# Late table clears, plain first-batch routing steps, and a reordered first expert group in an attention, expert and dense-FFN kernel

## The chip, the cores and the metric

One core of one Trainium2 chip runs the whole program. The metric is the device time of one execution in microseconds. Three runs of the kernel before gave 405.20, 402.61 and 406.21 us, median 405.2. The engines are PE (matrix), DVE (vector), ACT (scalar), POOL (GpSimd) and SP, which here issues nearly all DMAs.

## The reference

```python
r = log1p(|i - j|) / log1p(max(i, 1))                       # 576 x 576
bias = relu(r[..., None] @ w1 + b1) @ w2                    # 32 hidden -> 8 heads
attn = softmax(q @ k.T / 8 + bias)                          # 2 batches, 8 heads, head size 64
x = (attn @ v), heads side by side                          # 1152 tokens x 512

e = argmax(x @ w_gate); gate = softmax(x @ w_gate)[e]       # 8 experts, capacity 288
# token i gets the next place of expert e; past the capacity its row stays 0
y = relu(x_e @ w1[e]) @ w2[e]                               # 512 -> 1024 -> 512
x[i] = gate[i] * y[place of i]

h = x @ w_in                                                # 512 -> 2048
out = (max(h, 0) + alpha * min(h, 0)) @ w_out               # 2048 -> 512
```

## The kernel before

**Attention** (0 to about 209 us) is the function `course`. Its PE, ACT and DVE instructions stand in the order in which the program is written (`tc.manual_schedule`); the order of SP's DMAs and of POOL is left to a scheduler. The bias of a block of rows is made on the way: `h` on ACT and DVE (L164, L166), `bps` on PE (L174), `st` on ACT (L182), which SP writes to a table `bd` in DRAM (L188) and reads back sheared as `bias` (L138). Attention itself runs in 24 steps over pairs of heads and row blocks: scores `sps` on PE (L242), bias and row maximum `p`, `mn` on DVE (L249), the exponential on ACT (L256), transposes (L284), values `av` (L301, L302). The table `LD` tells which loads each step issues; what has been written there later stands later in SP's queue, and SP works its queue in order.

**Clears.** Expert input rows lie in a DRAM buffer `xd`, output rows in `out`. Before anything is scattered into them they are cleared from a tile `zr` of zeros: four DMAs into `xd` (L122) and three into `out` (L125), one in each of the steps 12 to 18 (L905, L906). POOL fills `zr` at the very start (L114, L115). In step 12 the constants `c` are loaded too (L907); DVE copies five columns of them into `gt` at L435.

**Routing** of one batch is a list of 14 steps (`routing`, L337 to L455): `logits`, `logits_rows`, `choose`, `highest`, `hot`, `ranks`, `slots`, `places`, `gates`, five `row` steps and `scatter`. `ranks` multiplies on PE into `rk` (L393 to L395), which takes one of the two PSUM buffers that `layer1` uses. `row` transposes a row block on PE (`xp`, L442), scales it on DVE (`xr`, L444) and copies gate and token beside it (L446). `scatter` writes the rows to their places in `xd` with POOL's indirect DMAs (L450). Every step is wrapped in `first(...)`, which gives what it issues a high priority. Batch 0 is routed inside attention, batch 1 in the first expert group.

**The first expert group** is `job` (L560), about 210 to 250 us: eight rounds `f`, each `layer1(f)` (12 matmuls, L572), ACT's `hh` (L574) and DVE's `hl` (L575), and 24 matmuls of `layer2(f-1)` (L582) that need them. The weights of a quarter are split into a high half on ACT (L501) and a low half on DVE (L502). `side(i)` calls what hangs at position `i`: batch 1's routing, then `joblist`, which on DVE (L459 to L494) makes the table `jl` of the groups that follow, then four conversions of dense-FFN weights (`ahead`: load L720 or L723, ACT L731, DVE L733 to L735). What follows needs `jl`: SP's loads of the next group's weights (`raw`, L512, L514) and rows (`xj`, L544), PE's transposes of those rows (`xjT`, L554), POOL's early split of the next weights (L533, L534). In this stage the scheduler orders all engines by priority and by its own times. Then come a second group with a rider (250 to 285 us) and the dense FFN (285 to 405 us).

Of the kernel before, what the change touches and what calls it, by code (L numbers as in the profile page):

```python
# [10 lines left out]
F32 = mybir.dt.float32  # L11
# [11 lines left out]
N, DM = B * S, H * D  # L23
# [5 lines left out]
RW = DM + 2  # L29
FEW = 96  # L30
TINY = 32
BIG = float(1 << 20)
# [7 lines left out]
def build(tc, nc, a):  # L40
    V, A, G, T, SY = nc.vector, nc.scalar, nc.gpsimd, nc.tensor, nc.sync
    with contextlib.ExitStack() as ctx:
# [5 lines left out]
        gp = pool(ctx, "gp")  # L48
# [61 lines left out]
        go, pick = c1[:, 346:386], c1[:, 386:450]  # L110
        c8v = c1[:, 136:176].rearrange("p (u e) -> p u e", e=8)
        wgb = c1[:, 218:346].rearrange("p (n e) -> p n e", e=32)
        zr = gp.tile([128, RW], F32, name="zr")
        G.memset(zr[:, 0:DM + 1], 0.0)  # L114
        G.memset(zr[:, DM + 1:RW], BIG)  # L115
        xd = dr.tile([XROWS, RW], F32, name="xd")

        def clear(r):

            if r < 12:  # L120
                n = XROWS // 12
                rows_of.other(SY.dma_start(xd[:].rearrange("(p r) w -> p r w", r=12)[:, r:r + 3],  # L122
                                           zr[0:n].unsqueeze(1).to_broadcast([n, 3, RW])))
            else:
                out_of.other(SY.dma_start(a["out"].rearrange("(p r) w -> p r w", r=9)[:, r - 12:r - 9],  # L125
                                          zr[:, 0:DM].unsqueeze(1).to_broadcast([128, 3, DM])))
# [178 lines left out]
        def first(f):  # L305
            with tc.high_priority():
                f()
# [29 lines left out]
        def routing(b):  # L337
# [101 lines left out]
            def row(u):  # L439
                t = ps1(pt, "xp")  # L440
                for hp in range(4):
                    T.transpose(t[:, 128 * hp:128 * hp + 128], xT[b][:, hp, 128 * u:128 * u + 128], ident)  # L442
                x = r.x[u] = raw.tile([128, RW], F32, tag="xr", name="xr", bufs=5)
                V.tensor_tensor(x[:, 0:DM].rearrange("p (h d) -> p h d", h=8), t.rearrange("p (h d) -> p h d", h=8),  # L444
                                r.rinv[:, u].unsqueeze(2).to_broadcast([128, 8, 64]), ALU.mult)
                V.tensor_copy(x[:, DM:RW], r.gt[:, u])  # L446

            def scatter():
                for u in range(5):
# [1 line left out]
                        out=xd[:], out_offset=bass.IndirectOffsetOnAxis(ap=r.ci[:, u:u + 1], axis=0),  # L451
                        in_=r.x[u], in_offset=None, bounds_check=XROWS - 1, oob_is_err=False))

            return [lambda f=f: first(f) for f in (logits, logits_rows, choose, highest, hot, ranks, slots, places, gates)
                    + tuple(lambda u=u: row(u) for u in range(5)) + (scatter,)]  # L455

        jl = gp.tile([128, 52], I32, name="jl")

# [90 lines left out]
        def job_transpose(ts, x, few=None):  # L549
            xh, xl = x  # L550
            for r in range(3):
                t = ps1(pt, "xjT")
                for d in range(4):
                    T.transpose(t[:, 96 * d:96 * d + 96], ts[r][:, 128 * d:128 * d + 128], ident[:96, :96])  # L554
                t = t[:, :384].rearrange("p (d r) -> p d r", d=4)
                halves(xh[:, :, 96 * r:96 * r + 96], xl[:, :, 96 * r:96 * r + 96], t)
                if few is not None and r == 0:
                    V.tensor_copy(few, t)

        def job(x, w0, raws, yo, side, engs=(None,) * 3):  # L560

            xh, xl = x
            acc = [pq.tile([128, 2, 512], F32, tag="pq", name="acc") for _ in range(2)]
            W = {0: w0}

            def layer1(f):
                w1h, w1l = [w.rearrange("p (k c) -> p k c", k=4) for w in W[f // 2][:2]]
                c = 128 * (f % 2)
                ps = ps1(pa, "g1")[:, :CAP]
                for k in range(4):  # L570
                    for i, (w, x_) in enumerate(((w1h, xh), (w1h, xl), (w1l, xh))):
                        T.matmul(ps, w[:, k, c:c + 128], x_[:, k], start=k + i == 0, stop=k + i == 5)  # L572
                hh, hl = [M.p.tile([128, 608], F32R, tag=n, name=n, bufs=3)[:, :CAP] for n in ("hh", "hl")]
                A.activation(hh, ps, AF.Relu)  # L574
                V.scalar_tensor_tensor(hl, ps, 0.0, hh.bitcast(F32), ALU.max, ALU.subtract)  # L575
                return hh, hl

            def layer2(f, hh, hl):
                w2h, w2l = [w.rearrange("p (f n) -> p f n", f=2)[:, f % 2] for w in W[f // 2][2:]]
                for d in range(4):  # L580
                    for i, (w, h) in enumerate(((w2h, hh), (w2h, hl), (w2l, hh))):
                        T.matmul(acc[d // 2][:, d % 2, :CAP], w[:, 128 * d:128 * d + 128], h, start=f == 0 and i == 0,  # L582
                                 stop=f == 7 and i == 2)

            prev = None
            for f in range(8):
                if f == 0:
                    W[1] = raw_split(1, raws[0], engs[0])
                h = layer1(f)
                side(2 * f)  # L590
                if prev:
                    layer2(f - 1, *prev)
                side(2 * f + 1)
                if f == Q3 and callable(raws[2]):
                    raws[2] = raws[2]()
                if f in (2, 4):
                    W[f // 2 + 1] = raw_split(f // 2 + 1, raws[f // 2], engs[f // 2])
                prev = h
            layer2(7, *prev)
            to_dense(acc, yo, CAP)  # L600
# [268 lines left out]
        raw = None  # L869
        NU = len(SL)  # L870
        late = []

        def course():
# [20 lines left out]
            LD = {s: [] for s in range(NU + 1)}  # L894
            for s, *x in ((0, load_bias, 0, 0), (0, load_bias, 0, 1), (1, load_bias, 0, 2), (1, load_bias, 0, 3),
# [6 lines left out]
                          (18, load, 1, 0), (19, load_bias, 2, 0), (19, load, 1, 1), (20, load_bias, 3, 0),  # L902
                          (21, load_bias, 2, 1), (21, load_bias, 3, 1)):
                LD[s].append(x)
            for s in range(12, 19):  # L905
                LD[s].append((clear, 3 * s - 36))  # L906
            LD[12] += [(lambda: SY.dma_start(c1, a["c1"]),), (rest_sums, 0)]  # L907
            LD[22].append((rest_sums, 1))

# [15 lines left out]
            for s in range(NU + 1):  # L925
# [9 lines left out]
                u, w = us[-1] if us else None, ws[-1] if ws else None  # L935
# [50 lines left out]
                else:  # L986
# [4 lines left out]
                    if w and w.small:  # L991
                        turn(w, 0)()
                        b = [blocks(1)]
                        turn(w, 4)()
                    elif w:
                        turn(w, 0, 1, 2, 3)('A')
                        turn(w, 4)('D')
                        b = [blocks(1)]
                    else:
                        b = [blocks(1)]  # L1000
# [14 lines left out]
                if s == 13:  # L1015
                    right.close()
                    raw = ctx.enter_context(tc.tile_pool(name="raw", bufs=1, side="right"))
# [47 lines left out]
        def prepare(r, at=9, late=False):  # L1065

            g = Unit()
            g.r, g.few, g.t = r, M.x[r % 2 if isinstance(r, int) else 0], None

            def tiles():  # L1070
                g.ts, g.x = row_tiles(), x_tiles(r == 1 if isinstance(r, int) else 0)

            def rows():
                if late:
                    tiles()
                    g.t = raw_tile(expert_of(r), 0)
                job_rows(g.ts, row_of(r, [ET.SP]))

            if not late:
                tiles()  # L1080
            g.todo = (at, rows), (14, lambda: job_transpose(g.ts, g.x, g.few))
            return g

        def group(g, few, side=lambda i: None, begin=lambda: None):
# [21 lines left out]
        def counts():  # L1106
            J.mode = nc.values_load(jl[0:1, 51:52], min_val=0, max_val=2, skip_runtime_bounds_check_because="a course")

        g1 = prepare(1, late=True)
        step = stepper(*zip((0, 1, 2, 2, 2, 3, 3, 3, 3, 4, 4, 4, 5, 5, 5), routing(1)), (6, lambda: first(joblist)), (7, counts),  # L1110
                       *((9 + i, lambda i=i: ahead(i)) for i in range(PRE)), *g1.todo)
        job(x0, w0, J.t0[1:], 0, step)
# [111 lines left out]
```

## Time and profile before

| | us |
|---|---|
| runs | 402.61, 405.20, 406.21 |
| the profiled execution | 406.84, span 405.0 |
| PE busy in the span | 375.8 (93%) |
| DVE, ACT, POOL busy | 284.2, 235.9, 29.3 |
| mean granted clock of PE | 0.987 of 2.4 GHz |

PE is busy for 93% of the span, so little of the time is idle; the table of windows tells in which stretches PE stood or ran at the lower clock. A row of a timeline gives start, duration, engine, line, operation, output, inputs, shape and count, and in brackets how long the engine was idle just before and for whom it waited. SPq is SP's queue: its duration is that of the issue, not of the transfer.

### The profile page before, as it was taken

To read this page: it belongs to the slowest core of one execution; us is meant where nothing else is said; L and a number is where in the kernel's file an instruction comes from. 1 tells how busy PE (TensorE), PEld (TensorE's weight loads), DVE (VectorE), ACT (ScalarE), POOL (GpSimd) and SP (SyncE) were. 2 spreads that over 40 slices of the span, in tenths; PEclk is the share of its full clock that TensorE was granted. 3 is DMA by queue.
4 is the path that set the end of the run, shared out by engine and by line. 5 is a ranking of instruction groups with operands and counts; after the bars stand their busy time and mean duration, and the time that the engine had idled before them with its cause. 6 is when DMAs were issued, how large, how long until landed. Compare 5 with 4: busy or idle time off the path is not lost. (4 is left out here: it accounts for less than half of the span.)

```text
span 405.0 us, 7529 instructions
## 1 busy us (share of the span) xinstructions
PE 375.8 (93%) x2728; PEld 274.0 (68%) x2729; DVE 284.2 (70%) x687; ACT 235.9 (58%) x518; POOL 29.3 (7%) x48
## 2 busy tenths in 40 slices
PE   4999997999999999999987997999999999999993
PEld 2424563546666656656656997878889898887982
DVE  5987975665656656776748897605999989887540
ACT  4876786776557655464644345515667657656531
POOL 2000000000000000012010522002000000000004
PEclk9999999899999999999999899999999999999998
DMA  7998899998997271341458179485345664540003
GB/s 302 292 288 276 282 356 251 320 311 301 400 326 272 87 251 43 108 142 36 119 170 242 59 214 324 138 279 153 112 155 179 180 207 146 168 158 3 0 0 129
DMA packets 44010, 78.77 MB, mean 195 GB/s; under 512 B 7127, under 2 KB 21591, under 8 KB 43964
## 3 DMA queue, kind: packets, MB, share of 16 engines
q1 hardware_dynamic: 42780, 75.73, 57.8%
q0 software_dynamic: 1184, 2.48, 1.7%
q8 instruction: 23, 0.38, 0.4%
q14 instruction: 23, 0.19, 0.2%
HBM read 59.50 MB, written 20.09 MB: 197 GB/s over the span
## 5 line engine op out<-in xcount | busy, mean ns | idle before, releaser
L249 DVE CUSTOM_DVE_ANT_0 p<-sps,bias 128x576 f32<-128x576 f32 x72 | 51.9, 754 | 23.6 <-PE sps L242 14.0
L256 ACT ACTIVATE p<-p,mn 128x576 f32<-128x576 f32 x72 | 55.7, 775 | 17.4 <-DVE mn L249 17.4
L174 PE MATMUL bps<-h,c 128*32 128x512 f32 (+17 forms) x352 | 39.5, 500 | 10.6 <-DVE h L166 5.4
L263 ACT COPY PT<-t 128x512 f32<-128x512 f32 (+2 forms) x52 | 27.5, 531 | 36.3 <-PE t L284 35.4
L166 DVE TENSOR_SCALAR h<-c 128x528 f32<-128x528 f32 (+17 forms) x126 | 46.4, 442 | 0.2
L284 PE MATMUL t<-ident,p 128*128 128x128 f32 x288 | 43.1, 282 | 2.8 <-ACT PT L263 1.5
L284 PEld LDWEIGHTS t<-ident,p 128*128 128x128 f32 x288 | 31.0, 141 | 20.8 <-ACT PT L263 9.0
L242 PE MATMUL sps<-kqv 64*128 64x288 f32 x256 | 43.3, 430 | 0.0
L806 PE MATMUL fg<-yh,w1l 128*128 128x304 f32 x120 | 36.3, 302 | 0.0
L806 PE MATMUL fg<-yh,w1h 128*128 128x304 f32 x120 | 36.2, 302 | 0.0
L806 PE MATMUL fg<-yl,w1h 128*128 128x304 f32 x120 | 36.2, 302 | 0.0
L182 ACT ACTIVATE st<-bps,c 128x527 f32<-128x527 f32 (+35 forms) x72 | 31.9, 510 | 7.0 <-PE bps L174 5.8
L301 PE MATMUL av<-PT,kqv 128*64 128x256 f32 (+1 forms) x320 | 33.5, 349 | 0.0
L731 ACT ACTIVATE cv<-d 128x512 f32<-128x512 f32 x32 | 21.6, 674 | 16.4 <-DMA d<-in_wout 7.8
L301 PEld LDWEIGHTS av<-PT,kqv 128*64 128x64 f32 x320 | 20.5, 140 | 15.6 <-issue 10.2
L242 PEld LDWEIGHTS sps<-kqv 64*128 64x128 f32 x256 | 25.2, 186 | 8.0 <-issue 2.7
L818 PE MATMUL facc<-w2h,hh 128*128 128x512 f32 (+1 forms) x75 | 29.8, 397 | 0.4 <-ACT hh L501 0.4
L818 PE MATMUL facc<-w2h,hl 128*128 128x512 f32 (+1 forms) x75 | 29.8, 398 | 0.3 <-DVE hl L502 0.3
L818 PE MATMUL facc<-w2l,hh 128*128 128x512 f32 (+1 forms) x75 | 29.6, 394 | 0.0
L174 PEld LDWEIGHTS bps<-h,c 128*32 128x32 f32 x352 | 11.5, 112 | 25.2 <-DVE h L166 8.4
L303 DVE COPY xT<-av 128x256 f32<-128x256 f32 (+2 forms) x28 | 9.2, 327 | 23.1 <-PE av L302 23.0
L501 ACT CAST hh<-g 128x304 fp32r<-128x304 f32 x32 | 14.3, 445 | 16.0 <-DVE g L810 15.8
(200 smaller groups left out, 768.8 us busy)
## 6 DMA issues: line engine op xcount, KB each, us to landing
bias<-bd SPq DMA_DIRECT2D x24, 576.0 KB, 5.9
kqv<-in_kqv SPq DMA_DIRECT2D x14, 864.0 KB, 6.5
bd<-st SPq DMA_DIRECT2D x36, 295.5 KB, 5.5
raw<-in_ew SPq DMA_DIRECT2D x16, 512.0 KB, 6.4
d<-in_win SPq DMA_DIRECT2D x16, 512.0 KB, 3.8
d<-in_wout SPq DMA_DIRECT2D x16, 512.0 KB, 3.8
w<-in_ew SPq DMA_DIRECT2D x6, 512.0 KB, 8.2
xd<-zr SPq DMA_DIRECT2D x4, 722.8 KB, 7.3
```

The source lines that it names most:

```text
L166: V.tensor_scalar(h, tab[:, :n], psi[:, i:i + 1], 0.0, ALU.add, ALU.max)
L174: T.matmul(ps[32 * c:32 * c + 32, n0:n1], w2n, hs[c][:, n0:n1], start=True, stop=True)
L182: A.activation(st[:, o:o + src.shape[1]], src, AF.Copy, scale=rr[:, t:t + 1])
L242: T.matmul(u.sc[ul, h][0][:, nh, :288], q[p, 128 * ul:128 * ul + 128], k[p, 288 * nh:288 * nh + 288], start=True, stop=True)
L249: V.tensor_tensor_reduce(out.rearrange("p (a b) -> p a b", a=2), ps[:, :, :288], bias.rearrange("p (a b) -> p a b", a=2), -0.125, 3.0e38, ...
L256: A.activation(out, out, AF.Exp, bias=mn, scale=-1.0, accum_out=acc)
L263: A.copy(o, i)
L284: T.transpose(t[:, jl, 128 * i:128 * i + 128], u.P[ul][:, 128 * j:128 * j + 128], ident)
L301: T.matmul(o[p, :n], v[:, j, p], rhs(h, j), start=j == 0, stop=False, skip_group_check=True)
L731: A.mul(v, r[:, :, 1].bitcast(F32), 2.0 ** -112)
L806: T.matmul(ps, w[:, 128 * k:128 * k + 128], x[:, k, s], start=k + i == 0, stop=k + i == 5)
L818: T.matmul(acc[i][:m], h[:, r:r + m], w, start=f == 0 and j == 0, stop=f == NF - 1 and j == 2)
```

## The change

Five edits. (1) `zr` is no longer filled at the start: it is made in another pool at the first clear. (2) The clears hang at steps 14 to 20 instead of 12 to 18. (3) Batch 0's routing steps lose the priority wrapper, and of batch 1's steps `gates` and the five `row` steps do. (4) In `job` the split of weight quarter 1 is written behind `layer1(0)` and `side(0)`. (5) The next group's loads hang at position 8 instead of 9, and its transposes at 15 instead of 14.

```diff
-        zr = gp.tile([128, RW], F32, name="zr")
-        G.memset(zr[:, 0:DM + 1], 0.0)
-        G.memset(zr[:, DM + 1:RW], BIG)
+        zr = None
         xd = dr.tile([XROWS, RW], F32, name="xd")
 
         def clear(r):
 
+            nonlocal zr
+            if zr is None:
+
+                zr = raw.tile([128, RW], F32, name="zr")
+                G.memset(zr[:, 0:DM + 1], 0.0)
+                G.memset(zr[:, DM + 1:RW], BIG)
...
-            return [lambda f=f: first(f) for f in (logits, logits_rows, choose, highest, hot, ranks, slots, places, gates)
-                    + tuple(lambda u=u: row(u) for u in range(5)) + (scatter,)]
+
+            return [(lambda f=f: first(f)) if b and i not in (8, 9, 10, 11, 12, 13) else f for i, f in enumerate(
+                    (logits, logits_rows, choose, highest, hot, ranks, slots, places, gates)
+                    + tuple(lambda u=u: row(u) for u in range(5)) + (scatter,))]
...
             for f in range(8):
+                h = layer1(f)
+                side(2 * f)
                 if f == 0:
                     W[1] = raw_split(1, raws[0], engs[0])
-                h = layer1(f)
-                side(2 * f)
...
-            for s in range(12, 19):
-                LD[s].append((clear, 3 * s - 36))
+            for s in range(14, 21):
+                LD[s].append((clear, 3 * s - 42))
...
-            g.todo = (at, rows), (14, lambda: job_transpose(g.ts, g.x, g.few))
+            g.todo = (at, rows), (15 if late else 14, lambda: job_transpose(g.ts, g.x, g.few))
...
-        g1 = prepare(1, late=True)
+        g1 = prepare(1, 8, late=True)
```

In attention the orders of PE, ACT and DVE stay as they were. Three places move. Lines of the changed kernel are 4 to 6 higher: its L126 is L122 here, L192 is L188, L913 is L907, L448 and L450 are L444 and L446, L508 is L502, L581 is L575, L739 to L741 are L733 to L735.

SP's queue around the load of the constants `c`, before:

```order
L188 DMA bd_117<-st 16x8x591 x2
L122 DMA xd<-zr 120x3x514
L907 DMA c_110<-in_c 128x450
L320 DMA rs_104<-rs_106 64x4x1 x2
L188 DMA bd_117<-st 16x8x591 x2
L122 DMA xd<-zr 120x3x514
L138 DMA bias<-bd_117 128x2x576 x2
```

and now, with the place where the first clears stand:

```order
L192 DMA bd_114<-st 16x8x591 x2
L913 DMA c_110<-in_c 128x450
L324 DMA rs_104<-rs_106 64x4x1 x2
L192 DMA bd_114<-st 16x8x591 x2
L142 DMA bias<-bd_114 128x2x576 x2
...
L142 DMA bias<-bd_115 128x2x576
L142 DMA bias<-bd_114 128x2x576
L126 DMA xd<-zr 120x3x514
L142 DMA bias<-bd_115 128x2x576
L199 DMA kqv<-in_kqv 128x1728
L126 DMA xd<-zr 120x3x514
```

No clear stands ahead of the constants any more; the clears stand between later loads of bias and heads.

DVE in the first expert group, from the end of batch 1's row products to the first two `hl`, before:

```order
L434 RECIPROCAL gt_2565<-sg 128x5
L1039 TENSOR_SCALAR malpha<-alpha 128x16
L386 SCALAR_TENSOR_TENSOR run<-c_110,eu 128x40
L446 COPY xr<-gt_2565 128x2 x5
L575 SCALAR_TENSOR_TENSOR hl<-g_2461,hh 128x288
L575 SCALAR_TENSOR_TENSOR hl<-g_2500,hh 128x288
L403 SCALAR_TENSOR_TENSOR kept_120<-thr,rk 128x8
```

and now, from the routing's first product on:

```order
L368 TENSOR_TENSOR lgt<-lgr,rinv_2470 128x320
L581 SCALAR_TENSOR_TENSOR hl<-g_2453,hh 128x288
L371 TENSOR_REDUCE L<-lgt 128x40
L1045 TENSOR_SCALAR malpha<-alpha 128x16
L508 TENSOR_TENSOR w2l<-raw,w2h 128x1024
L376 TENSOR_REDUCE mx<-L 128x5
L581 SCALAR_TENSOR_TENSOR hl<-g_2500,hh 128x288
L378 TENSOR_TENSOR m<-L,mx 128x40
```

The two `hl` come ahead of the row products; three products now stand ahead of `kept` and two far behind it, in `joblist`.

DVE at the end of the same group, around the last three `hl`, before:

```order
L735 SCALAR_TENSOR_TENSOR cw<-d,cw 128x512
L734 SCALAR_TENSOR_TENSOR ah_2762<-cv,ah_2762 128x512
L733 TENSOR_SCALAR ah_2762<-cv 128x512
L502 TENSOR_TENSOR ah_2761<-cw,ah_2761 128x512
L735 SCALAR_TENSOR_TENSOR ah_2762<-d,ah_2762 128x512
L575 SCALAR_TENSOR_TENSOR hl<-g_2844,hh 128x288
L734 SCALAR_TENSOR_TENSOR ah_2762<-cv,ah_2762 128x512
L735 SCALAR_TENSOR_TENSOR ah_2762<-d,ah_2762 128x512
L575 SCALAR_TENSOR_TENSOR hl<-g_2880,hh 128x288
L502 TENSOR_TENSOR xl<-xjT,xh 128x4x96
```

and now:

```order
L581 SCALAR_TENSOR_TENSOR hl<-g_2798,hh 128x288
L739 TENSOR_SCALAR cw<-cv 128x512
L739 TENSOR_SCALAR ah_2779<-cv 128x512
L740 SCALAR_TENSOR_TENSOR cw<-cv,cw 128x512
L740 SCALAR_TENSOR_TENSOR ah_2779<-cv,ah_2779 128x512
L741 SCALAR_TENSOR_TENSOR cw<-d,cw 128x512
L741 SCALAR_TENSOR_TENSOR ah_2779<-d,ah_2779 128x512
L581 SCALAR_TENSOR_TENSOR hl<-g_2844,hh 128x288
L508 TENSOR_TENSOR ah_2778<-cw,ah_2778 128x512
L581 SCALAR_TENSOR_TENSOR hl<-g_2880,hh 128x288
L508 TENSOR_TENSOR xl<-xjT,xh 128x4x96
```

Six conversions stand in one run ahead of `hl(6)`; the last conversion's three operations moved from ahead of `hl(7)` to between the `xl`. SP's `d<-in_wout` load for that last conversion now stands behind the `raw` and `xj` loads instead of ahead of them.

## Rows read from the trace of the kernel before

**Rows 1.** Windows by stage: busy us of PE, PEld, DVE, ACT, POOL, clock, DMA share, GB/s.

```profile
57.00:84.00 27.00, 23.81 (x204) 13.41 (x200) 17.24 (x53) 19.00 (x44) 0.00 (x0) 0.94 0.96 288
209.00:252.00 43.00, 38.05 (x275) 35.23 (x271) 36.57 (x93) 18.72 (x31) 12.10 (x9) 0.96 0.64 193
```

**Rows 2.** Timeline of steps 12 to 14: start, duration, work, idle time before and releaser.

```profile
58.21 1.40 PE L242 MATMUL sps<-kqv 64*128 64x288 f32 x8
58.99 1.29 SPq L122 DMA_DIRECT2D xd<-zr  x1
60.33 0.45 SPq L907 DMA_DIRECT2D c<-in_c  x1
63.87 1.36 PE L242 MATMUL sps<-kqv 64*128 64x288 f32 x8
66.35 0.17 DVE L435 COPY gt<-c 128x5 f32<-128x5 f32 x1 [4.21 <-DMA c<-in_c]
68.82 0.88 PE L174 MATMUL bps<-h,c 128*32 128x400 f32 x8 [2.90 <-DVE mn L249]
74.06 1.24 PE L242 MATMUL sps<-kqv 64*128 64x288 f32 x8
```

**Rows 3.** DMA issues by name, 57 to 75 us: count, size, median us to landing.

```profile
xd<-zr SPq DMA_DIRECT2D x4, 722.8 KB, 7.3
```

**Rows 4.** Windows inside the stages: idle stretches, and those at the lower clock.

```profile
70.00:73.30 3.30, 3.30 (x25) 1.63 (x25) 2.16 (x6) 2.62 (x6) 0.00 (x0) 0.50 0.92 280
223.60:226.90 3.30, 3.30 (x16) 3.30 (x15) 2.98 (x12) 0.00 (x0) 0.51 (x1) 0.50 0.00 0
243.10:246.40 3.30, 1.07 (x10) 0.86 (x10) 3.23 (x3) 0.89 (x2) 2.20 (x1) 1.00 1.10 304
```

**Rows 5.** Timeline of the first expert group.

```profile
221.25 0.81 DVE L575 SCALAR_TENSOR_TENSOR hl<-g,hh 128x288 fp32r<-128x288 f32 x2
221.75 0.42 PE L393 MATMUL rk<-run,ones 128*128 128x40 f32 x2 [2.33 <-DVE hl L575]
227.62 0.46 DVE L575 SCALAR_TENSOR_TENSOR hl<-g,hh 128x288 fp32r<-128x288 f32 x1 [1.04 <-ACT hh L574]
235.56 0.18 DVE L494 CAST jl<-jlst 128x52 int32<-128x52 f32 x1
245.16 0.55 PE L554 MATMUL xjT<-ident,xj 96*128 96x96 f32 x4 [2.06 <-DMA xj<-xd]
245.77 0.45 DVE L575 SCALAR_TENSOR_TENSOR hl<-g,hh 128x288 fp32r<-128x288 f32 x1
249.87 0.30 PE L572 MATMUL g<-xh,w1h 128*128 128x288 f32 x1
```

**Rows 6.** POOL's split of the next weights and the DVE operations beside it.

```profile
241.51 1.04 POOL L533 CAST w1h<-raw 128x1024 fp32r<-128x1024 f32 x1 [7.79 <-DVE ah L735]
241.70 1.40 DVE L734 SCALAR_TENSOR_TENSOR ah<-cv,ah 128x512 int32<-128x512 int32 x1
242.64 2.66 POOL L534 TENSOR_TENSOR w1l<-raw,w1h 128x1024 fp32r<-128x1024 f32 x1
243.13 2.71 DVE L735 SCALAR_TENSOR_TENSOR ah<-d,ah 128x512 int32<-128x512 int32 x1
```

**Rows 7.** Other conversions by line: count, ns least, median, most, first and last start.

```profile
L733 DVE TENSOR_SCALAR cw<-cv x30: 415/420/573, 228.3 to 367.7; 128x512 int32<-128x512 int32 x30
L735 DVE SCALAR_TENSOR_TENSOR cw<-d,cw x30: 679/683/693, 232.2 to 372.8; 128x512 int32<-128x512 int32 x30
```

**Rows 8.** Line L188, the writes of the bias table: count, ns, first and last start.

```profile
L188 SPq DMA_DIRECT2D bd<-st x36: 517/524/897, 9.3 to 91.9; - x36
```

**Rows 9.** Window of attention at 100 to 120 us.

```profile
100.00:120.00 20.00, 19.50 (x160) 12.69 (x160) 11.48 (x30) 12.04 (x29) 0.58 (x2) 1.00 0.98 358
```

**Rows 10.** DMA issues by name, 95 to 150 us: count, size, median us to landing.

```profile
kqv<-in_kqv SPq DMA_DIRECT2D x7, 864.0 KB, 5.3
out<-zr SPq DMA_DIRECT2D x1, 768.0 KB, 9.6
```

## The prediction, made before the changed kernel ran

> **What bounds the kernel now.** PE is busy for 93% of the span, so time can only come back where PE stands, where it runs at the lower of its two clock levels, or where another engine holds it. I read the windows by stage first. From 57 to 84 us PE is busy 23.81 of 27.00 us at a granted clock of 0.94, and from 209 to 252 us 38.05 of 43.00 at 0.96, with DVE at 36.57 [rows 1]. These are the stretches the change touches. Inside the dense FFN and the second group it moves nothing that I can see, and I take them as unchanged.
>
> Then the timeline of steps 12 to 14. A step is the time from one first score matmul to the next. The step from 58.21 takes 5.66 us, the step from 63.87 takes 10.19 [rows 2]: 4.53 us too long. Two rows say why. DVE's copy of `c` columns into `gt` waits 4.21 us for the DMA of the constants, until 66.35; behind it on DVE stand `h` and the row maxima, so PE waits 2.90 us before `bps` at 68.82 [rows 2]. After that PE runs at half clock (0.50, that is 1.2 GHz) for about 3.3 us, with PE busy all of it [rows 4]; that is worth up to half, 1.65 us. 2.90 + 1.65 = 4.55, which fits the 4.53.
>
> Last, the timeline of the first expert group. PE waits 2.33 us at `rk` for `hl(0)`, which stands on DVE at 221.25 behind batch 1's row products; then PE runs at 0.50 from 223.6 to 226.9 [rows 4, 5]. Near the end PE waits 2.06 us for the rows `xj` [rows 5], without a fall of the clock behind it (1.00 in the window 243.1 to 246.4) [rows 4]. But DVE is nearly full there: 2.98 of 3.30 us in the half-clock stretch, 3.23 of 3.30 at the end [rows 4], and its largest wait after `rk` is 1.04 us [rows 5]. So in the second half of this group DVE sets the pace, and PE time won early is mostly lost again.
>
> **The change, part by part.**
>
> *Clears off the constants' queue.* The constants were issued at 60.33 behind one clear of `xd` issued at 58.99 [rows 2]; now they follow `bd` directly. The issue moves up by 1.34 us. The transfer ahead of them, 722.8 KB [rows 3], is 2.6 us at this stretch's 288 GB/s [rows 1]. So the constants land 1.34 us earlier if only the issue counts, 2.6 us if the DMA engines work in order of issue; I take 2.2, nearer the second, since the DMA share there is 0.96 [rows 1] and an issue in a full queue waits for the bytes ahead. DVE's 4.21 becomes about 2.0, and PE's 2.90 about 0.7. A pause of 0.7 us is much shorter than those of 2.33 and 2.90 that preceded the two half-clock stretches, and shorter than the 2.06 that did not [rows 2, 4, 5], so I let that stretch go as well, but count only 1.1 of its 1.65 us because ACT and DVE were busy 2.62 and 2.16 of 3.30 there [rows 4] and do not get faster with PE. **Attention: -3.3 us.** Bounds: -1.3 (issue only, clock still halves) and -4.5 (whole excess).
>
> *Clears at steps 14 to 20, `zr` made late.* Four transfers of 722.8 KB and three of 768 KB go from a full stretch into the one up to about 150 us. At 100 to 120 us the DMA engines are at 0.98 with 358 GB/s [rows 9], yet PE is busy 19.50 of 20.00 there, though one `out` clear with 9.6 us to landing already stands among the loads [rows 9, 10]. The heads' loads land after 5.3 us [rows 10] and are issued a step or more ahead. The loads also lose the clears that were ahead of them. I take 0. Bounds: -0.5 (the idle PE time in that window) and the slower rival below. POOL fills `zr` on an engine idle there, 0.58 of 20 us busy [rows 9]; what waits for it is SP, and that is the rival's place. The fill that goes from the start was on POOL alone and is worth 0.
>
> *Priorities of batch 0.* The order of PE, ACT and DVE in attention is that of the program and does not move: 0.
>
> *`gates` and row products of batch 1 lose priority; the split is written later.* `hl(0)` and `hl(1)` now stand right behind the routing's first product. PE's 2.33 us at `rk` goes: `rk`'s PSUM buffer is free early, and PE has 23 matmuls of `layer2` ahead of it instead of 2. What is late next is DVE. Up to `hl(7)` its list loses the three operations of the last conversion, which now stand among the `xl`: 0.42 + 0.68 + 0.68 = 1.8 us at their usual durations [rows 7]. Of its idle 1.04 us [rows 5] some goes too. `hl(7)` was at 245.77 and the next group began at 249.87 [rows 5]. So -1.8 to -2.8 for `hl(7)`. Part returns behind it: the same three operations now delay the last `xl`, which the next group's first matmuls need, and ACT's step for that conversion waits for a weight load that SP now issues behind the loads of the next group's weights and rows. Between +0.5 (all returned and PE slowed) and -2.8, I take **-1.5 us**, nearest to the shorter list less a little. The half clock after `rk` I don't add: DVE was full beside it.
>
> *Loads at position 8, transposes at 15.* `jl` was written at 235.56 [rows 5]. Two operations of 0.68 us and perhaps the 1.04 of waiting no longer precede it, so it is ready 1.4 to 2.4 us sooner, and `xj` with it. The wait of 2.06 for `xj` was hidden, as PE needed `hl(7)` at about the same time. Counted at 0; if it were not hidden it is part of the -2.8.
>
> Sum: -3.3 - 1.5 = -4.8 us. The profiled execution took 406.84 (span 405.0 and 1.8 around it), so 402.0 for such an execution. It lies 1.64 above the median of the three runs, 405.2; against that: **400.4 us**.
>
> **A rule that speaks against it.** POOL splits the next weights in 1.04 and 2.66 us, and the two DVE conversions beside it took 1.40 and 2.71 us [rows 6] where 0.68 is usual [rows 7]: 0.72 + 2.03 = 2.75 us lost. The second of them started at 243.13 and ended at 245.84, 0.54 after POOL's at 245.30 [rows 6], so it did not run beside it but behind it. The Trainium skill, page "SBUF — State Buffer", section "Who interferes with whom", says that a DVE instruction with two SBUF inputs and a GpSimd instruction that reads SBUF never overlap, and that the later one is blocked for the whole of the other. The trace agrees (0.54 us left to do against 0.68 alone). By the rule up to all of POOL's 3.7 us could fall on DVE rather than 2.75, and the sum would be -3.8.
>
> **Rivals.**
>
> *The blockade moves onto PE's path.* Before, the 2.75 us fell ahead of `hl(7)` while PE waited 2.06 us for `xj` anyway. With `jl` 1.4 to 2.4 us earlier, POOL's split starts earlier, beside the run of six conversions ahead of `hl(6)`: 2 x 0.42 + 4 x 0.68 = 3.6 us alone [rows 7], 6.3 with 2.75 on top. PE has 24 matmuls of `layer2` meanwhile, about 2.5 us (16 took 3.30 at half clock [rows 4], so 24 take 2.5 at full). PE stands up to 3.8 us there, which is longer than the pauses after which the clock fell to 0.50, and then up to 1.65 us more goes. First group -1.5 + 1.65 = +0.2; total -3.1, **402.1**. For it: rows 6 and the new order. Against: DVE paid the same price before. Chance 0.17.
>
> *Everything returns.* Attention -4.5, first group -2.8: -7.3, **397.9**. For it: no work that the pauses waited for is left in front of it in its queue. Against: DVE full at the end. Chance 0.20.
>
> *The constants stay late.* Their landing may be set by the `bd` transfers and the shared engines rather than by the clear. Attention -1.3, total -2.8, **402.4**. For it: 0.96 DMA share; against: 2.6 us of bytes less ahead. Chance 0.12.
>
> *Slower: SP stands at the first clear.* SP's first clear waits for POOL's fill of `zr`, and the fill waits until the memory of the bias tiles is free, after the last `bd` lands: the last two are issued up to 91.9 us [rows 8] and land some us later. Bias and head loads are queued behind it. If SP reaches it about 10 us too early, the loads behind are 10 us late; once that exceeds the roughly 5 us by which loads are ahead of use (they land in 5.3 [rows 10]) plus the 4.8 won, time is lost. A step stalled twice by 5 us gives +10 - 4.8 = +5.2, **410.4**. Against: the clear stands in the queue behind bias loads that wait for that same last `bd`, so SP should get there late. Chance 0.07.
>
> **How the numbers follow.** 1% of 405.2 is 4.05 us, about what a measurement of this kernel can tell from no change, so faster means under 401.15. My forecast has 0.44, between -3.3 and -5.9; 0.31 of that is past the bound, 0.13 within. Faster: 0.31 + 0.20 = 0.51. Same: 0.13 + 0.17 + 0.12 = 0.42. Slower: 0.07. The range goes from 397.4 (everything, and the 0.5 of the DMA-bound window) to 404.2 (-1.0: attention -1.3 with the first group at +0.3); the slower rival and small tails stay out.
>
> **What would show it.** The copy into `gt` should wait about 2 us instead of 4.2, `bps` behind it under 1, and the step from about 63.9 should last about 7 us or less at clock 1.00. `rk` should start without a wait over 1 us. Attention should end near 206 instead of 209 us. POOL's split should lie ahead of 241.5 less the attention's gain, and if DVE's conversions ahead of `hl(6)` show 1.4 and 2.7 us with PE idle beside them, the first rival holds. The next group should begin at 244 to 246 instead of 249.87. I am wrong if bias or head loads end a PE wait over 1 us between 90 and 150 us, if the step of the constants still takes 9 us, or if the stages after 252 move by more than 1 us.

## The result, and the profile after

The changed kernel took 398.77 us (median of four runs, 398.37 to 403.35) against 405.7 of the kernel before (402.61 to 407.12): ratio 0.986, interval 0.982 to 0.990. In a later set beside other kernels it took 396.61, ratio 0.977 (0.972 to 0.982). The forecast was 400.4, faster. The sign and the two places were right, the size was short: -4.8 us from the 405.2 of the three runs before, against -6.9 here and -9.6 in the later set, whose 396.61 lies below the 397.4 at which the range began.

Its profiled execution took 398.69 us with a span of 396.9, against 406.84 and 405.0. Read by stage, from the first matmul of the first expert group and of the group behind it (before, the first of the two was the line below, the second stands in [rows 5]):

```profile
210.47 0.48 PE L572 MATMUL g<-xh,w1h 128*128 128x288 f32 x1
```

| stage | before | after | difference |
|---|---|---|---|
| attention | 210.47 | 206.47 | -4.00 |
| first expert group | 39.40 | 34.86 | -4.54 |
| second group and dense FFN | 155.13 | 155.57 | +0.44 |

The last line is untouched code; in the fourteen profiles of this study it lies between 153.2 and 156.4. One profile's total is therefore no measure of 1 us. A stage is a better one, with limits: five profiles with the changed attention (changed, e7, e9, e10, e11) end it between 205.93 and 207.30, and five with the changed first group (changed, e3, e6, e8, e9) take 34.36 to 34.93 for it.

The windows of the changed kernel, in the columns of [rows 1] and [rows 4]:

```profile
57.00:84.00 27.00, 25.92 (x231) 14.96 (x227) 19.75 (x59) 22.00 (x51) 0.00 (x0) 1.00 0.69 221
120.00:150.00 30.00, 29.92 (x216) 19.15 (x216) 17.81 (x44) 17.98 (x44) 0.23 (x1) 1.00 0.90 311
205.00:241.00 36.00, 34.85 (x258) 31.80 (x254) 30.41 (x88) 16.51 (x28) 14.19 (x9) 1.00 0.61 189
```

Full clock in all three, and 25.92 us of PE work where there were 23.81. The DMA share went from 0.96 to 0.69 in the first. The clears' bytes turn up from 100 us on: the second window moves 311 GB/s where the kernel before moved 191, and PE is busy for 29.92 of its 30 us (29.90 before). The same window before:

```profile
120.00:150.00 30.00, 29.90 (x215) 19.49 (x215) 19.07 (x46) 18.43 (x44) 0.00 (x0) 1.00 0.57 191
```

Steps 12 to 14 in its timeline, beside [rows 2]:

```profile
58.00 1.40 PE L246 MATMUL sps<-kqv 64*128 64x288 f32 x8
58.70 1.37 SPq L913 DMA_DIRECT2D c<-in_c  x1
63.66 1.35 PE L246 MATMUL sps<-kqv 64*128 64x288 f32 x8
63.91 0.17 DVE L439 COPY gt<-c 128x5 f32<-128x5 f32 x1 [1.98 <-DMA c<-in_c]
66.38 0.88 PE L178 MATMUL bps<-h,c 128*32 128x400 f32 x8 [0.68 <-DVE mn L253]
70.06 1.30 PE L246 MATMUL sps<-kqv 64*128 64x288 f32 x8
```

The copy waits 1.98 instead of 4.21, PE 0.68 instead of 2.90, and the step lasts 6.40 instead of 10.19. The forecast had about 2.0, 0.7 and 7 or less. The line of the clears into the row buffer (count, ns, first and last start) tells where they went, from 59.0 to 74.2 before to:

```profile
L126 SPq DMA_DIRECT2D xd<-zr x4: 437/499/1237, 99.2 to 119.2; - x4
```

The first expert group, beside [rows 5, 6]:

```profile
206.47 0.48 PE L578 MATMUL g<-xh,w1h 128*128 128x288 f32 x1
216.61 0.41 PE L397 MATMUL rk<-run,ones 128*128 128x40 f32 x2
228.87 0.18 DVE L500 CAST jl<-jlst 128x52 int32<-128x52 f32 x1
233.14 0.42 DVE L739 TENSOR_SCALAR ah<-cv 128x512 int32<-128x512 int32 x1
233.17 3.69 POOL L539 CAST w1h<-raw 128x1024 fp32r<-128x1024 f32 x1 [6.57 <-DMA raw<-in_ew]
233.48 0.69 DVE L740 SCALAR_TENSOR_TENSOR cw<-cv,cw 128x512 int32<-128x512 int32 x1
235.28 0.69 DVE L741 SCALAR_TENSOR_TENSOR ah<-d,ah 128x512 int32<-128x512 int32 x1
235.88 0.45 DVE L581 SCALAR_TENSOR_TENSOR hl<-g,hh 128x288 fp32r<-128x288 f32 x1
236.25 1.16 DVE L508 TENSOR_TENSOR ah<-cw,ah 128x512 fp32r<-128x512 f32 x1
236.95 2.71 POOL L540 TENSOR_TENSOR w1l<-raw,w1h 128x1024 fp32r<-128x1024 f32 x1
237.33 0.45 DVE L581 SCALAR_TENSOR_TENSOR hl<-g,hh 128x288 fp32r<-128x288 f32 x1
241.33 0.37 PE L578 MATMUL g<-xh,w1h 128*128 128x288 f32 x1 [0.50 <-ACT xh L507]
```

`rk` starts without a wait, and no pause over 0.5 us is left in the group. The surprise stands in the POOL rows: POOL's cast took 3.69 us where it took 1.04 before, while the six DVE conversions beside it kept their 0.42 and 0.68. Before, DVE paid for the collision; now POOL pays most of it, on an engine nobody waits for, and DVE only the 0.50 us by which the conversion at 236.25 is longer than usual.

### The profile page after: what moved, and what is told of

Same layout as the page of the kernel before. It is cut to its first block, busy times and chain, and to the rows that moved or that the text cites. A ratio compares the mean times of both kernels' runs of the same rounds, so it can differ in the third digit from the quotient of the medians.

```text
span 396.9 us, 7534 instructions
## 1 busy us (share of the span) xinstructions
PE 373.5 (94%) x2728; PEld 272.5 (69%) x2729; DVE 281.2 (71%) x687; ACT 234.8 (59%) x518; POOL 31.4 (8%) x48
## 5 line engine op out<-in xcount | busy, mean ns | idle before, releaser
L178 PE MATMUL bps<-h,c 128*32 128x512 f32 (+17 forms) x352 | 38.5, 495 | 8.4 <-DVE h L170 5.2
```

Source lines behind the costliest of these rows:

```text
L178: T.matmul(ps[32 * c:32 * c + 32, n0:n1], w2n, hs[c][:, n0:n1], start=True, stop=True)
```

## The experiments

Ratios are to the kernel before, with 95% intervals. The diffs of e1, e2, e3 and e5 are against the kernel before, those of the others against the changed kernel. One table for all, read from the profiles as above: attention's end, length of the first group, how long after the group's start its `hl(7)` starts, and what DVE's conversions ahead of `hl(7)` took above their usual duration beside POOL's split.

| kernel | ratio | attention | group | hl(7) | DVE excess |
|---|---|---|---|---|---|
| before | 1 | 210.47 | 39.40 | 35.30 | 2.75 |
| changed | 0.986 | 206.47 | 34.86 | 30.86 | 0.50 |
| e1 | 0.988 | 207.40 | 38.76 | 35.04 | 2.54 |
| e2 | 0.996 | 206.13 | 38.71 | 33.57 | 2.54 |
| e3 | 0.991 | 210.74 | 34.93 | 30.52 | 0.48 |
| e4 | 0.990 | 206.70 | 39.02 | 35.92 | 2.79 |
| e5 | 0.994 | 206.47 | 38.63 | 35.04 | 2.54 |
| e6 | 0.982 | 205.91 | 34.46 | 30.50 | 0.48 |
| e7 | 0.988 | 207.30 | 36.23 | 30.36 | 0.00 |
| e8 | 0.981 | 206.68 | 34.36 | 30.36 | 0.51 |
| e9 | 0.977 | 206.39 | 34.82 | 30.83 | 0.51 |
| e10 | 0.980 | 205.93 | 34.96 | 30.98 | 0.48 |
| e11 | 0.979 | 206.08 | 34.33 | 30.88 | 0.48 |
| e12 | 0.987 | 205.79 | 39.82 | 35.59 | 2.28 |

**e1, only the clears' part.**

```diff
-        zr = gp.tile([128, RW], F32, name="zr")
-        G.memset(zr[:, 0:DM + 1], 0.0)
-        G.memset(zr[:, DM + 1:RW], BIG)
+        zr = None
...
+            if zr is None:
+
+                zr = raw.tile([128, RW], F32, name="zr")
...
-            for s in range(12, 19):
-                LD[s].append((clear, 3 * s - 36))
+            for s in range(14, 21):
+                LD[s].append((clear, 3 * s - 42))
```

> Only the clears move (steps 14 to 20, zeros made at the first clear); the first expert group is as before. Theory A (the constants no longer stand behind a clear): the step of the constants falls from 10.2 to about 6.2 us at full clock, attention ends 4.0 us earlier than before, the expert group keeps its 39.4 us, total -4.0 us, ratio about 0.990. Rival B (the stages trade: what attention wins is waited away in the expert group, whose DMAs and clock depend on it): attention -4.0, total -2 or less, ratio above 0.995.

402.32 us, 0.988 (0.983 to 0.994). Attention ended 3.07 us earlier in its profile, the group took 38.76. A holds for the total, and PE kept full clock there; the step of the constants took 7.43 us instead of A's 6.2, as PE waited 1.70 us and not 0.68. The constants landed 0.26 us later than in the changed kernel, and on DVE the copy stands two `h` operations earlier, so that 0.67 us more of them come behind it:

```profile
60.74 0.42 DVE L170 TENSOR_SCALAR h<-c 128x400 f32<-128x400 f32 x1
64.17 0.17 DVE L439 COPY gt<-c 128x5 f32<-128x5 f32 x1 [3.01 <-DMA c<-in_c]
67.31 0.88 PE L178 MATMUL bps<-h,c 128*32 128x400 f32 x8 [1.70 <-DVE mn L253]
```

The changed kernel has three `h` there ahead of the copy (60.83, 1.09 us).

**e3, only the first group's part** (the other hunks of the change).

> Only the first expert group changes (priorities of gates and row products, split of quarter 1 later, loads at 8 and transposes at 15); clears and constants as before. Theory A (the two parts of the change are independent): attention as before with its 10.2 us step, the group takes about 35 us instead of 39.4, total -4 to -4.5, ratio about 0.989. Rival B (the group was short only because the profiled run kept full clock): the group takes 36.5 us or more, total -1.5 to -3, ratio 0.993 to 0.996.

402.44 us, 0.991 (0.988 to 0.994). Attention as before, group 34.93. A holds for the stages. Its profile kept full clock in the group too, so B is answered by the total alone: -3.7 us, beyond B's -3, with an interval that just touches B's 0.993. 1.2% for e1 and 0.9% for e3 add up to 2.1%, between the 1.4% and the 2.3% of the changed kernel's two sets.

**e2, the constants ahead of the first clear.**

```diff
+            LD[12] += [(lambda: SY.dma_start(c1, a["c1"]),), (rest_sums, 0)]
             for s in range(12, 19):
                 LD[s].append((clear, 3 * s - 36))
-            LD[12] += [(lambda: SY.dma_start(c1, a["c1"]),), (rest_sums, 0)]
```

> As before, but the constants are issued ahead of the first clear, and the clears stay at steps 12 to 18. Theory A (what counts is the clear ahead of the constants in the queue): DVE's copy waits about 2 us instead of 4.2, the row maxima and bps behind it come under 1 us late, attention -3.5 to -4.0 us, ratio about 0.991. Rival B (the stretch from 57 to 92 us is short of DMA bandwidth, so the clears must leave it): the copy's wait may fall, but other waits stay, attention -1.3 to -2, ratio 0.995 to 0.997.

**e5, only the table of steps.**

```diff
-            for s in range(12, 19):
-                LD[s].append((clear, 3 * s - 36))
+            for s in range(14, 21):
+                LD[s].append((clear, 3 * s - 42))
```

> Of the attention part only the table of steps changes (clears at 14 to 20); the zeros are made at the start, as before, and the first expert group is as before. In SP's order the clears stand from just behind the constants on, as with the constants first. Theory A (what holds the clears back to 100 us is that the zeros are made late; the table alone only lets the constants pass the first clear): clears are issued from about 61 us on, the copy waits about 2 us, PE under 1, time 402 to 404.5 us with more spread from run to run than the changed kernel, ratio 0.990 to 0.997. Rival B (the table moves the clears): clears issued from about 75 us on or later, times as with the whole attention part, ratio 0.988.

e2: ratio 0.996 (0.992 to 0.999), profiled run 400.15 us. e5: 402.57 us, 0.994 (0.991 to 0.997), profiled run 400.18. The two have the same order of instructions on every engine, so they are one kernel timed twice. In e2's profile the copy waits 1.60 us and PE 0.29; e2's stage is A's and its ratio B's, e5 is A's in both. In e5's timeline the clears follow right behind the constants:

```profile
57.35 1.32 SPq L188 DMA_DIRECT2D bd<-st  x2
58.73 1.37 SPq L907 DMA_DIRECT2D c<-in_c  x1
60.21 1.70 SPq L320 DMA_DIRECT2D rs<-rs  x2
62.02 0.59 SPq L122 DMA_DIRECT2D xd<-zr  x1
62.97 2.55 SPq L188 DMA_DIRECT2D bd<-st  x2
63.24 0.17 DVE L435 COPY gt<-c 128x5 f32<-128x5 f32 x1 [1.98 <-DMA c<-in_c]
```

So the new step numbers do not bring the clears to 100 us: making the zeros late does. The step numbers only let the constants pass the first clear, and in both profiles that alone gave attention its whole 4 us. By the ratios it is only 0.4 and 0.6%, 1.7 and 2.6 us: most of the compared runs took 402 to 405 us at a mean clock of 0.982 to 0.991, where the two profiled ones had 0.994 and 0.993. Whether the clears that stay in this stretch cost such runs their clock no profile caught, and e1's interval overlaps these. That part stays open.

**e4, row products keep their priority.**

```diff
-            return [(lambda f=f: first(f)) if b and i not in (8, 9, 10, 11, 12, 13) else f for i, f in enumerate(
-                    (logits, logits_rows, choose, highest, hot, ranks, slots, places, gates)
-                    + tuple(lambda u=u: row(u) for u in range(5)) + (scatter,))]
+            return [lambda f=f: first(f) for f in (logits, logits_rows, choose, highest, hot, ranks, slots, places, gates)
+                    + tuple(lambda u=u: row(u) for u in range(5)) + (scatter,)]
```

> The changed kernel, but gates and row products of batch 1 keep their high priority. Theory A (the row products on DVE ahead of hl(0) held PE at rk and brought the half clock behind it): PE waits over 1.5 us at rk again, the group takes 38 us or more, against the kernel before -4.5 us, ratio about 0.989. Rival B (the later split of quarter 1 or the earlier loads made the group short): the group takes about 35 to 36 us, ratio 0.980 to 0.983 against the kernel before.

401.9 us, 0.990 (0.984 to 0.996). The edit gives batch 0's steps their priority back too; attention ends at 206.70 all the same. The group takes 39.02, as A had it, but not by A's wait: `rk` waits 0.57 us and the next `layer1` 1.71, with the half clock behind it (0.50 from 220.8 to 224.2). In its timeline:

```profile
217.14 0.42 PE L397 MATMUL rk<-run,ones 128*128 128x40 f32 x2 [0.57 <-DVE run L390]
219.69 0.40 PE L577 MATMUL g<-xh,w1h 128*128 128x288 f32 x1 [1.71 <-DVE hl L580]
...
238.07 0.42 DVE L738 TENSOR_SCALAR ah<-cv 128x512 int32<-128x512 int32 x1
238.13 1.25 POOL L538 CAST w1h<-raw 128x1024 fp32r<-128x1024 f32 x1 [9.43 <-DMA raw<-in_ew]
238.52 1.42 DVE L739 SCALAR_TENSOR_TENSOR ah<-cv,ah 128x512 int32<-128x512 int32 x1
...
239.48 2.67 POOL L539 TENSOR_TENSOR w1l<-raw,w1h 128x1024 fp32r<-128x1024 f32 x1
...
239.97 2.73 DVE L740 SCALAR_TENSOR_TENSOR ah<-d,ah 128x512 int32<-128x512 int32 x1
242.62 0.44 DVE L580 SCALAR_TENSOR_TENSOR hl<-g,hh 128x288 fp32r<-128x288 f32 x1
```

POOL came 31.4 us into the group instead of 26.7, met the last conversion ahead of `hl(7)`, and DVE paid 2.79 us again.

**e6, constants at the start.**

```diff
                 if k == 10:
                     load_vd(0)
+                    SY.dma_start(c1, a["c1"])
...
-            LD[12] += [(lambda: SY.dma_start(c1, a["c1"]),), (rest_sums, 0)]
+            LD[12].append((rest_sums, 0))
```

> The changed kernel with the constants loaded in the first 10 us of the program, so that DVE's copy waits for nothing. Theory A (what is left of the wait, 1.98 us on DVE and 0.68 on PE, is on PE's path): attention another 0.6 us shorter, 398.1 us, ratio 0.984. Rival B (the early load delays the first heads by its 225 KB, or the next late load takes the place of the wait): no gain or up to 0.7 us loss, ratio 0.986 to 0.988.

397.13 us, 0.982 (0.978 to 0.986). The wait is gone, and attention ends 0.56 us sooner than in the changed kernel's first profile, as A has it. But e10, with its constants where the changed kernel has them, ends attention at 205.93, so the 0.56 is not told apart from the spread of that stage. Nor is the total: the changed kernel's 0.986 and 0.977 lie on both sides.

**e7, no early split on POOL.**

```diff
-                w0 = raw_split(0, t, early=True)
+                w0 = raw_split(0, t)
```

> The changed kernel, but POOL no longer makes the next group's first weight halves; ACT and DVE make them instead. Theory A (in the changed kernel POOL, not DVE, pays for the collision, so POOL's work is nearly free): DVE's conversions keep 0.68 us, the second group begins no earlier and then lacks its weights, 1 to 3 us slower than the changed kernel, ratio 0.989 to 0.993 against the kernel before. Rival B (the collision still costs DVE and PE about 1 us or more): the group ends 0.5 to 1 us earlier, ratio 0.982 to 0.986.

400.02 us, 0.988 (0.983 to 0.993). DVE's excess is 0.00, yet `hl(7)` is only 0.50 us earlier, and the next group then waits 1.99 us for ACT's `w1h`. A holds for the group: POOL's slow cast costs less than taking it away. The ratio alone does not tell e7 from the changed kernel's first set (0.982 to 0.990), only from its later one.

**e8, the row buffer cleared twice.**

```diff
+            for s in range(14, 18):
+                LD[s].append((clear, 3 * s - 42))
```

> The changed kernel with the four clears of the row buffer issued twice at steps 14 to 17 (the same zeros written again, 2.9 MB more). Theory A (loads in 95 to 150 us have several us to spare, so clears there cost nothing): at most 0.5 us more, ratio 0.985 to 0.988 against the kernel before. Rival B (the stretch is at its limit, and one more clear ahead of a load is waited for): 2.5 us per clear ahead of a load that is waited for, 3 to 10 us more, ratio 0.994 to 1.01.

397.06 us, 0.981 (0.977 to 0.986). Another 2.9 MB, issued from 99.4 to 140.6 us, cost nothing that can be seen: PE is busy for 54.39 of the 55 us from 95 to 150, in this kernel and in the changed one. A holds, B is refuted.

**e9, the changed kernel again.**

> The changed kernel once more, beside the kernels of this set. Theory (it holds full clock because no pause of 2.3 us or more is left on PE): 397.5 to 399 us, mean granted clock 0.995 or more in most runs, ratio 0.981 to 0.986. Rival (its first time was lucky): 400 us or more, ratio above 0.988.

396.61 us, 0.977 (0.972 to 0.982); clock 0.996 or more in five of six runs. The rival falls; the time lies 0.9 us below the theory's own range.

**e10, the split written early** and **e11, positions back.**

```diff
             for f in range(8):
+                if f == 0:
+                    W[1] = raw_split(1, raws[0], engs[0])
                 h = layer1(f)
                 side(2 * f)
-                if f == 0:
-                    W[1] = raw_split(1, raws[0], engs[0])
```

> The changed kernel with the split of weight quarter 1 written ahead of layer1(0) again. On DVE one low half of 1.2 us goes ahead of hl(0), and on PE eight xp transposes go ahead of the second half of layer2(0). Theory A (the priorities of the row products carry the gain of the first group): at most 1 us more, ratio 0.982 to 0.988. Rival B (the split order carries it): PE waits over 1.2 us for hl(0) and the half clock returns, 2 to 4 us more, ratio 0.990 or above.

```diff
-            g.todo = (at, rows), (15 if late else 14, lambda: job_transpose(g.ts, g.x, g.few))
+            g.todo = (at, rows), (14, lambda: job_transpose(g.ts, g.x, g.few))
...
-        g1 = prepare(1, 8, late=True)
+        g1 = prepare(1, late=True)
```

> The changed kernel with the next group's loads at position 9 and its transposes at 14. All eight first xjT transposes go ahead of most of layer2(6) on PE. Theory A (the rows xj are there in time now, but not two microseconds sooner): PE waits 1 to 2 us for xj before xjT, total 1 to 2 us more, ratio 0.986 to 0.991. Rival B (rows land early enough since jl is 6.7 us earlier): no difference, ratio 0.981 to 0.986.

e10: 398.3 us, 0.980 (0.976 to 0.985), group 34.96 with 0.55 us of waiting for `hl(0)`. e11: 397.69, 0.979 (0.975 to 0.984), group 34.33, without the 0.50 us at the next group's start. B holds for e11, and A for e10 by the group's length and clock; e10's median lies 1.7 us above that of e9 in the same set, more than A's 1 and less than B's 2, with intervals that overlap. Neither edit by itself is needed for the group's gain. A kernel with both taken back and the priorities kept as changed was not run.

**e12, conversions earlier, on e6.**

```diff
...
-                       *((9 + i, lambda i=i: ahead(i)) for i in range(PRE)), *g1.todo)
+                       *((7 + i, lambda i=i: ahead(i)) for i in range(PRE)), *g1.todo)
```

> The changed kernel with the constants loaded at the start and the four conversions hung at positions 7 to 10 instead of 9 to 12, so that the last weight load goes ahead of the next group's loads and all conversions ahead of hl(7). Theory A (the next group starts 0.8 us late because ACT's cv and the last conversion stand among its xh and xl): first group 0.5 to 1 us shorter, 396.3 us, ratio 0.978 to 0.982. Rival B (conversions ahead of hl(5) to hl(7) hold PE, DVE being full there): first group 0.5 to 2.5 us longer, ratio 0.984 to 0.988.

400.68 us, 0.987 (0.983 to 0.992). A failed. The conversions went ahead of a low half that the next `layer1` needs; PE waited, and the clock stayed at half for twice as long as elsewhere, as its timeline and window show:

```profile
232.74 0.40 PE L578 MATMUL g<-xh,w1l 128*128 128x288 f32 x1 [1.78 <-DVE w1l L508]
235.44 0.61 PE L588 MATMUL acc<-hl,w2h 128*128 128x288 f32 x1 [0.60 <-DVE hl L581]
```

```profile
233.50:240.00 6.50, 5.90 (x26) 5.55 (x25) 6.17 (x7) 0.41 (x1) 3.52 (x2) 0.51 1.06 300
```

B was right, and its price for the group too low: the group is 5.4 us longer than in e6. In its excess of 2.28 us, 0.47 fell on a conversion with one input, 1.81 on one with two:

```profile
235.31 0.89 DVE L739 TENSOR_SCALAR ah<-cv 128x512 int32<-128x512 int32 x1
```

## Why the prediction was right or wrong

*Clears off the constants' queue:* right in mechanism and place, -4.0 against -3.3. The copy's wait fell by 2.23 us and PE's by 2.22, the 2.2 that was taken. The half-clock stretch went wholly: 10.19 - 6.40 = 3.79 for the step, so all of its 1.6 and not 1.1. The step of the working that failed is that ACT and DVE beside it would keep part of it. The other 0.21 us of the 4.00 is already there where the step begins (63.87 and 63.66).

*Clears late:* 0, as forecast; e8 doubles those into the row buffer and sees nothing.

*Priorities of batch 0:* worked out as 0, because no order would move. From the kernel before to the changed one none does. But e1, e2, e4 and e5 keep this priority with no clear ahead of the constants, and there DVE's copy stands two `h` earlier: from the copy to `bps` it takes 3.14 to 3.15 us, in the changed kernel 2.47. So of the change's -4.0 in attention up to 0.67 us hangs on this edit, wherever the copy comes late.

*Row products behind `hl`:* right in place and direction, the term was mis-sized, -4.5 against -1.5. The group shrank by what `hl(7)` moved, 4.44 of 4.54, and nothing came back behind it (4.00 us to the next group, 4.10 before). Two steps of the working gave too little.

The first left the 2.75 us of the collision with POOL on DVE. It fell to 0.50, because POOL's cast came 4.34 us earlier in the group, beside the run of conversions ahead of `hl(6)`, where POOL lost. 2.69 us of these are the earlier `jl`; the rest is `raw`, issued 0.73 us behind `jl` instead of 1.04 and followed by the cast after 3.57 us instead of 4.91, now that SP's load of `d` is issued behind it. e4 shows which edit does it: without the lower priority of the row products POOL comes 4.7 us later and DVE pays. In the table every group of 34 to 35 us has an excess of 0.5 and every group over 38 has 2.3 or more.

The second is "The half clock after `rk` I don't add: DVE was full beside it". e2 and e5 are one kernel, with DVE's order in this group as before. Behind the same wait at `rk`, e5 ran at 0.50 and e2 at 1.00. e5, a window and the starts of the group, `hl(2)` and `hl(7)`:

```profile
219.00:220.00 1.00, 1.00 (x6) 1.00 (x6) 1.00 (x6) 0.00 (x0) 0.00 (x0) 0.50 0.00 0
206.47 0.48 PE L572 MATMUL g<-xh,w1h 128*128 128x288 f32 x1
223.61 0.46 DVE L575 SCALAR_TENSOR_TENSOR hl<-g,hh 128x288 fp32r<-128x288 f32 x1 [1.03 <-ACT hh L574]
241.51 0.45 DVE L575 SCALAR_TENSOR_TENSOR hl<-g,hh 128x288 fp32r<-128x288 f32 x1
```

and e2:

```profile
219.00:220.00 1.00, 1.00 (x10) 1.00 (x9) 1.00 (x3) 0.00 (x0) 0.00 (x0) 1.00 0.01 2
206.13 0.48 PE L572 MATMUL g<-xh,w1h 128*128 128x288 f32 x1
222.18 0.45 DVE L575 SCALAR_TENSOR_TENSOR hl<-g,hh 128x288 fp32r<-128x288 f32 x1
239.70 0.45 DVE L575 SCALAR_TENSOR_TENSOR hl<-g,hh 128x288 fp32r<-128x288 f32 x1
```

DVE was full inside the half-clock stretch, but behind it `hl(2)` waited 1.03 us for `hh`, which waits for PE's `g`. In e2 that wait is not there; `hl(2)` starts 1.09 us sooner and `hl(7)` 1.47 (33.57 against 35.04). So the 1.04 us that DVE waited before belongs to the half clock, and PE time won early was not lost again by `hl(7)`. (e2 lost it behind `hl(7)`, where its own clock fell.) Beside e2, with full clock up to `hl(7)` in both, the new order is worth 2.71 us and not 4.44, of which the collision is 2.54 - 0.50 = 2.04. The 1.8 us of the shorter list do not appear in full: `hl(5)` starts 0.67 us later in the changed kernel than in e2. This division rests on differences of single profiles; no run takes the collision alone out of the order before.

*The rival of the blockade* had the place right, beside the six conversions, and the loser wrong. *Everything returns* was nearest, 397.9, partly by luck: it had -4.5 for attention and -2.8 for the group, 1.7 us too little there, and the profiled execution fell by 8.15 us where the medians fell by 6.9. *The slower rival* did not arise: POOL had filled `zr` by 92.07, SP issued the first clear at 99.15, and PE had no wait over 1 us between 90 and 150 us.

*The step numbers:* I ascribed the clears' new place to them and the late zeros together. e5 separates them.

## What to carry over

When two engines collide on a shared resource, moving one of them can change who pays; look for the engine that nobody waits for, and price both outcomes. A small load that an in-order engine waits for should not stand behind bulk clears in the queue, and a table of steps moves a DMA only if nothing else, like the time at which its source is ready, holds it. Price a stretch at half clock by what waits for PE's results behind it, not only by how busy the next engine is inside it. Read a change of 1% by stage, since untouched stages of a single profile differ by 3 us here.

## What the runs showed of the hardware

Length of a pause does not by itself foretell the half clock here. The 2.33 us at `rk` was followed by 0.50 in the kernel before, in e1 and in e5; in e2 the same pause was followed by full clock, and the fall came at 240, behind a pause of 1.33:

```profile
218.00:222.00 4.00, 4.00 (x32) 4.00 (x32) 3.71 (x18) 0.41 (x1) 0.00 (x0) 1.00 0.03 12
240.00:243.50 3.50, 3.50 (x18) 3.49 (x18) 1.57 (x5) 0.96 (x2) 0.00 (x0) 0.51 1.07 372
```

The pauses of 1.71 (e4), 1.78 (e12) and 1.99 (e7, with one of 1.48 behind it) were followed by one too, those of 2.06 (before) and 1.70 (e1) not. My reasoning from pause lengths was too simple; where the clock falls was seen, not explained.

In the collision of POOL and DVE the record's start does not tell who goes first. POOL's cast is recorded from 233.17, ahead of the conversion at 233.48, and still ran behind the run of conversions: it ended at 236.86, 0.98 us after the start of `hl(6)` at 235.88, which is about the 1.04 that it needs alone. `hl` reads one operand from PSUM and one from SBUF. In e12 `hl(5)`, at 234.94 beside POOL's cast of 1.09 us, kept its 0.45 too. In e4 POOL's cast started at 238.13, and the conversion at 238.52 waited. In both traces the cast is recorded 0.03 to 0.06 us behind the start of a one-input conversion (233.14, 238.07), and a two-input one follows; the outcome is opposite. Here the Trainium skill, page "SBUF — State Buffer", section "Who interferes with whom", says that the order of issue decides which of the two blocks the other. Both traces agree that one of them is blocked wholly; which one it was could not be read from the recorded starts, and what decides it stays open.

A conversion with one input can pay as well: 0.89 us instead of 0.42 beside POOL's cast in e12.
